# A decode kernel (attention with a cache, and a mixer MLP): weight loads moved in the DMA order, four column tiles with one fold, scores lagging four blocks

## Chip, cores, metric

One core of one Trainium2 chip. The metric is the device time of one execution in microseconds (us); lower is better. A "span" is the time from the first to the last instruction in the profile; it is about 1.7 us below the device time of the same run.

## The reference, cut to what matters

```python
x = A_x; xn = layernorm(x)                                   # 4 rows of 576
q = (xn @ wq)                                                # 32 heads of 128
k, v = last 2048 rows of the caches                          # 16 kv heads, 2 q heads each
attn = softmax(q k^T / sqrt(128)) v @ wo
h  = gelu(layernorm(xn) @ w1)                                # goes into zeros: S = 1, all four shifts are padding
x1 = xn + shifted(h) @ w2
mlp = x1 + gelu(layernorm(x1) @ w3) @ w4
out = x + attn + mlp
```

The data are 88.5 MB: K and V 33.6 MB each in 16 chunks of 2.097 MB, wq 4.7, w3 5.3, wo 4.7, w4 5.3, w1 and w2 1.3 together.

## The kernel before

Every operation is entered with a key, and each engine runs its operations in the order of the keys. PE (TensorE) is in order too: an operation that waits stops all behind it. This is what the argument needs:

```python
# --- DMA: the sync engine's queue unless engine= says otherwise ---
ev_x  = add_dma([(x_sb, x2)], "x", (), -100, engine="act")
ev_w1 = add_dma([(w1main, ...), (w1rag, ...)], "w1", (), -60)
ev_w2 = add_dma([(w2main, ...), (w2rag, ...)], "w2", (), -59)
ev_wq = [add_dma([(kt_t, ...)], "wq", (), -20), add_dma([(wqrag, ...)], "wqr", (), -15)]
for c in range(16):   # ring of 4 slots: chunk c waits until chunk c-4 has been transposed
    add_dma([(ring_pos(c), K chunk c)], ("k", c % 4), [t_done(c - 4)] if c >= 4 else [], c)
for c in range(16):   # V uses the same ring
    add_dma([(ring_pos(c), V chunk c)], ("v", c % 4), [f"PV{c-4}" if c >= 4 else t_done(c + 12)], KS + c)
ev_w3 = ... key W3_KEY = 140        # behind K15, ahead of V0 (KS = 144)
ev_wo = ... waits ["h2_4"], key KS + 15.5   # into w3's bytes, so w3 must have been read: behind V15
# w4 in five parts of 18, 10, 5, 2, 1 rows, behind wo

# --- PE, in the order of the keys ---
# xT(-40)  hs = hs_inT @ w2 (-39)  x2T(-36)  hT = w1.T xn2T (-35)  x1T(-34)  q = wq.T xnT (-30)  zeroing  K loop
for c in range(16):
    for k in range(8):                       # 8 blocks of 8 transposes, 4 PSUM buffers
        if k < 2 or k >= 4: wait(copy of the block four back)
        transpose block k                    # VectorE or ScalarE copies it out
        if k == 1: wait(copies 6 and 7 of chunk c-1); scores of chunk c-1   # SC_AFTER = 1
# max, exp, transposes of P, t1, then
# h2 = w3.T x1nT: 180 products (waits "PT3"), then 16 x PV
# AO: for r in 32: for h in 2: acc[h] += ORT[:, :, r].T @ wo[r, half h]      # 64 products, 4 stationary columns
# w4: for t in 36: for h in 2: acc[h] += h2T[:, t].T @ w4[t, half h]         # 72 products, 4 stationary columns
```

... (norms, masks, softmax details and the output are cut)

Of the kernel before, what the change touches and what calls it, by code (L numbers as in the profile page):

```python
# [5 lines left out]
FP32 = mybir.dt.float32  # L6
BF16 = mybir.dt.bfloat16
ACTF = mybir.ActivationFunctionType
ALU = mybir.AluOpType
AX = mybir.AxisListType  # L10
# [2 lines left out]
NPOS = 4  # L13
ACT_EVAC = (1, 4, 7)
N_WARM = 6
W3_KEY = 140.0
WO_AT = 15.5
W4_ROWS = (18, 10, 5, 2, 1)


# [14 lines left out]
def bass_parallel_sum__sliding_block_cached__mixer_s_mlp__decode_kernel(  # L35
    nc, A_x, A_k_cache, A_v_cache, A_wq, A_wo, B_x, B_w1, B_w2, B_w3, B_w4, out
):
    B, Sq, D = A_x.shape
# [10 lines left out]
    NBLK = NT // 8  # L49
# [3 lines left out]
    HALF = D // 2  # L53
# [6 lines left out]
    with ExitStack() as ctx:  # L60
        def sb(name, shape, dt):
            return ctx.enter_context(nc.sbuf_tensor(name, shape, dt))
# [9 lines left out]
        PT_t = sb("PT", [128, NT * 32], BF16)  # L72
# [4 lines left out]
        PTx = kt_t[:, 2048:4096].rearrange("p (q x) -> p q x", q=4)  # L77
# [4 lines left out]
        wo_v = w3_t[:, 0:32 * D].rearrange("p (r n) -> p r n", r=32)  # L82
        w3r = [w3_t[:, r * F:(r + 1) * F] for r in range(4)]
        w3rag = w3_t[:, 4 * F:4 * F + FH]
        w1main = w4_t[:, 0:4 * D].rearrange("p (r n) -> p r n", r=4)
        w1rag = w4_t[:, 4 * D:4 * D + HALF]
        w2main = w4_t[:, 5 * D:9 * D].rearrange("p (r n) -> p r n", r=4)
        w2rag = w4_t[:, 9 * D:9 * D + HALF]
# [13 lines left out]
        x1nT = sb("x1nT", [128, 6, B], BF16)  # L102
        hs_inT = sb("hs_inT", [128, 6, B], BF16)
        hT_sb = sb("hT_sb", [128, len(HCH), B], BF16)
        h2T_sb = sb("h2T_sb", [128, 36, B], BF16)
# [5 lines left out]
        permT_bf = sb("permT_bf", [128, 128], BF16)  # L111
        ident_f = sb("ident_f", [128, 128], FP32)
# [4 lines left out]
        zeros_bf = sb("zeros_bf", [128, 512], BF16)  # L117
# [7 lines left out]
        OTy = sb("OTy", [128, B, 32], BF16)  # L125
        ORT = sb("ORT", [128, B, 32], BF16)
        t1 = sb("t1", [B, D], FP32)
        out_sb = x1n_bf

        ps = ctx.enter_context(nc.psum_tensor("ps", [128, 8, 512], FP32))[:]  # L130
# [3 lines left out]
        ORps = ps[:, 2, 0:128]  # L134
        rinvps = ps[:, 3, 0:128]
        OTps = ps[:, 6, 0:32]
        H2Tps = ps[:, 7, 0:144].rearrange("p (c b) -> p c b", b=B)
        QTps = ps[:, 7, 0:128]
        HSps = [ps[0:B, k, 0:HALF] for k in range(2)]
# [10 lines left out]
        def add(engine, emit, waits=(), sig=None, key=0.0, inc=(), loop=None, cond=None):  # L150
            seqc[0] += 1
            prog[engine].append(Op(emit, waits, sig, key, seqc[0], inc, loop, cond))
# [6 lines left out]
        def take(nm, n=1):  # L159
            return ("take", tok(nm), n)  # L160

        def add_dma(pairs, skey, waits=(), key=0.0, engine="sp"):
            tok(skey)
            dma_count[skey] = dma_count.get(skey, 0) + 16 * len(pairs)

            def emit(e):
                for o_, i_ in pairs:
                    e.dma_start(o_, i_).then_inc(S[skey], 16)
            add(engine, emit, waits, None, key)
            return ("dma", skey, dma_count[skey])  # L170

        def rag_src(w_ap):
            return w_ap[512:576, :].rearrange("r (h n) -> (r h) n", h=2)

        KS = float(NB + 16)
# [26 lines left out]
            add("dve", lambda e, x=x: e.tensor_copy(out=mU_bf[:, :, x], in_=mU[:]), waits=["mU"], sig=f"mU_bf{x}", key=-7.8)  # L202


        ev_x = add_dma([(x_sb[:], x2)], "x", (), -100, engine="act")
        ev_w1 = add_dma([(w1main, B_w1[0:512, :].rearrange("(p r) n -> p r n", r=4)), (w1rag, rag_src(B_w1))], "w1", (), -60)
        ev_w2 = add_dma([(w2main, B_w2[0:512, :].rearrange("(p r) n -> p r n", r=4)), (w2rag, rag_src(B_w2))], "w2", (), -59)
        ev_wq = [add_dma([(kt_t[:], A_wq[0:512, :].rearrange("(p r) n -> p (r n)", r=4))], "wq", (), -20),
                 add_dma([(wqrag, rag_src(A_wq))], "wqr", (), -15)]

# [122 lines left out]
        def pe_SC(c):  # L333
            def f(e):
                ins = None
                for q in range(4):
                    for u in range(NU):
                        ins = e.matmul(Sps[32 * u:32 * u + 32, q, :].rearrange("p (t i) -> p t i", t=16),  # L338
                                       lhsT=Qs[:, c % NPOS, 32 * u:32 * u + 32], rhs=ktgrp[:, 4 * (c % 2) + q, :, u, :],
                                       start=False, stop=True, tile_position=(0, 32 * u), skip_group_check=True)  # L340
                return ins
            return f

        SC_AFTER = 1
        evtok = lambda k: take("evA" if k in ACT_EVAC else "evD")
        for c in range(NC):
            lp = ("K", c // NPOS)
            for k in range(NBLK):
                w = [take(("k", c % NPOS), 16)] if k == 0 else []
                prev = (k + 4) % 8  # L350
                if k < 2 or k >= 4:
                    w.append(evtok(prev))
                add("pe", pe_T(NBLK * c + k), waits=w, sig=f"T{NBLK * c + k}", key=NBLK * c + k, loop=lp)
                eng, f = evac(NBLK * c + k)
                add(eng, f, waits=[f"T{NBLK * c + k}"] + ([f"SC{c - 2}"] if c >= 2 else []), inc=[("evA" if eng == "act" else "evD", 1)],
                    key=NBLK * c + k + 0.2)
            add("pe", pe_SC(c - 1), waits=[evtok(6), evtok(7), take("qs")], sig=f"SC{c - 1}", key=NBLK * c + SC_AFTER + 0.5, loop=lp)
            b, gq = CH[c]
            cc = 4 * b + gq
            P(lambda e, c=c, cc=cc: e.tensor_copy(out=Qs[:, c % NPOS, :], in_=Qpad_t[:, 128 * cc:128 * cc + 128]),  # L360
              waits=["qT", "qs_zero"] + ([f"SC{c - NPOS}"] if c >= NPOS - 1 else []), inc=[("qs", 1)], key=c)
# [12 lines left out]
        for q in range(4):  # L374
            k0 = KS + 0.2 + 0.1 * q
            add("dve", lambda e, q=q: e.transpose(out=PTx[:, q, :], in_=P_sb[:, q, :]), waits=[f"exp{q}"], sig=f"PTx{q}", key=k0)  # L376
            add("pe", lambda e, q=q: e.matmul(ps[:, 4 + q, :], lhsT=permT_bf[:], rhs=PTx[:, q, :], start=True, stop=True),  # L377
                waits=[f"PTx{q}", "permT_bf"], sig=f"PTy{q}", key=k0)
            add("act", lambda e, q=q: e.activation(out=PT_t[:, 512 * q:512 * (q + 1)], in_=ps[:, 4 + q, :], func=ACTF.Copy),
                waits=[f"PTy{q}"], sig=f"PT{q}", key=k0 + 0.16)  # L380
        add("dve", lambda e: e.tensor_reduce(out=rsum[:], in_=rs4[:], axis=AX.X, op=ALU.add), waits=["exp3"], sig="rsum", key=KS + 0.8)
        add("dve", lambda e: e.reciprocal(out=rinv[:], in_=rsum[:]), waits=["rsum"], sig="rinv", key=KS + 0.81)
# [37 lines left out]


        def acc_mm(e, h, lhsT, rhs, start=False, stop=False):
            return e.matmul(ACC[h], lhsT=lhsT, rhs=rhs, start=start, stop=stop)  # L423

        def pe_AO(e):
            ins = None
            for r in range(32):
                for h in range(2):
                    ins = acc_mm(e, h, ORT[:, :, r], wo_v[:, r, HALF * h:HALF * (h + 1)])
            return ins  # L430
        KH = -58.0
        add("dve", lambda e: e.transpose(out=OTy[:].rearrange("p b r -> p (b r)"), in_=OTn[:]), waits=["OTn3"], sig="OTy", key=KT - 3)  # L432
# [45 lines left out]
        def pe_h2(r):  # L478
            def f(e):
                ins = None  # L480
                for n, (lo, hi, st) in enumerate(w4cols):
                    if r < 4:
                        ins = e.matmul(H2Tps[:, n, :], lhsT=w3r[r][:, lo:hi:st], rhs=x1nT[:, r, :],  # L483
                                       start=(r == 0 and n == 0), stop=False, skip_group_check=True)
                    else:
                        h = lo // FH
                        ins = e.matmul(H2Tps[:, n, :], lhsT=w3rag[:, lo - FH * h:hi - FH * h:st], rhs=x1nT[:, 4 + h, :],
                                       start=False, stop=True, skip_group_check=True)
                return ins
            return f  # L490
        for r in range(5):
            add("pe", pe_h2(r), waits=[ev_w3[r // 4]] + (["x1nT", "PT3"] if r == 0 else []), sig=None if r == 3 else f"h2_{r}",
                inc=[("otn", 1)] if r == 3 else [], key=KS + 2 + 0.1 * r)
        add("act", lambda e: e.activation(out=h2T_sb[:], in_=H2Tps, func=ACTF.Gelu_apprx_tanh), waits=["h2_4"], sig="gelu2", key=KS + 3)

        last_p = len(W4N) - 1
        for n, (t0, t1_) in enumerate(W4N):
            def f(e, t0=t0, t1_=t1_, hs=(0, 1), n=n):
                ins = None
                for t in range(t0, t1_):  # L500
                    for h in hs:
                        ins = acc_mm(e, h, h2T_sb[:, t, :], w4tile[t][:, HALF * h:HALF * (h + 1)], stop=(t == 35))
                return ins
            if n < last_p:
                add("pe", f, waits=[ev_w4[n], "gelu2"], sig=f"MO{n}", key=KT + 20 + n)
            else:
                for h in range(2):
                    add("pe", lambda e, f=f, h=h: f(e, hs=(h,)), waits=[ev_w4[n], "gelu2"], sig=f"MOl{h}", key=KT + 20 + n + 0.1 * h)
        add("dve", lambda e: e.tensor_copy(out=out_sb[:, 0:HALF], in_=ACC[0]), waits=["MOl0"], sig="fin0", key=KT + 50)  # L509
        add("act", lambda e: e.activation(out=out_sb[:, HALF:D], in_=ACC[1], func=ACTF.Copy), waits=["MOl1"], sig="fin1", key=KT + 50)  # L510

# [103 lines left out]
```

## Time and profile before

| | before |
|---|---|
| device time | 233.9 us (232.87 to 234.39, 3 runs) |
| profiled run | 236.5 us, span 234.8 |
| bytes at the V phase's rate (428.6 GB/s) | 206.5 us |
| end of the stream of loads | about 224.1 us |

The profile's lines are in the prediction below. The DMA row shows that the kernel is a stream of loads with a hole near 137 us and a tail of 10.7 us without loads. One more view: the timeline of the first 60 us of the kernel before. Columns of the timeline: start, length, engine, line, instruction, count, and in brackets the idle time before it and what ended it.

```profile
8.23 0.56 PEld L461 LDWEIGHTS ps<-w,hs_inT 128*4 128x4 bf16 x4 [2.56 <-DMA w<-in_B_w_dram]
...
34.14 25.23 SPq L168 DMA_DIRECT2D ring<-in_A_k_cache_dram  x5
```

The product with w2 (hs) starts at 8.23. K4 is issued at 34.14, when chunk 0 has been transposed; this moment is called T(0) below.

### The profile page before, as it was taken

The page shows a single profiled execution, that of the slowest core. Times are in us where ns is not written, and L with a number is a line of the kernel's source. Part 1 is how long each engine was busy: PE and PEld are TensorE (multiplying, and loading weights), DVE is VectorE, ACT ScalarE, POOL GpSimd, SP SyncE. Part 2 cuts the span into 40 slices and gives each one's busy share as a digit, 9 for nine tenths or more (in the row PEclk, how much of TensorE's full clock was granted, in tenths as well). Part 3 has the DMA queues.
Part 4 walks back from the last instruction along what each step waited for, and adds up shares of the span by engine and source line. Part 5 has one row for each costly group of instructions (what it writes and reads, how often), then busy time and mean ns, then how long its engine had stood idle before and what let it go on. Part 6 is the DMA issues. An engine that isn't in the chain of part 4 may idle for free. (4 is left out here: it accounts for less than half of the span.)

```text
span 234.8 us, 6313 instructions
## 1 busy us (share of the span) xinstructions
PE 156.7 (67%) x2874; PEld 126.0 (54%) x2876; DVE 75.5 (32%) x147; ACT 59.4 (25%) x71; POOL 10.6 (5%) x35
## 2 busy tenths in 40 slices
PE   0519898599989999999619996334433344306996
PEld 0218377477777777777504996334433344303664
DVE  4521165436665566666564002000110100100000
ACT  2020056246566555656656000000000000000000
POOL 8100000000000000000000000000000000000000
PEclk9999999979999999999965555555555555555999
DMA  6999999988999999999899919999999999999910
GB/s 202 432 392 437 430 424 422 395 332 329 402 388 399 366 371 363 392 461 446 374 442 436 413 56 396 430 438 422 433 441 416 433 424 430 474 394 421 409 40 1
DMA packets 6659, 88.67 MB, mean 378 GB/s; under 512 B 748, under 2 KB 1144, under 8 KB 1912
## 3 DMA queue, kind: packets, MB, share of 16 engines
q1 hardware_dynamic: 6632, 88.50, 91.5%
q8 instruction: 9, 0.15, 0.2%
q14 instruction: 2, 0.02, 0.0%
q10 hardware_dynamic: 16, 0.01, 0.0%
HBM read 88.49 MB, written 0.00 MB: 377 GB/s over the span
## 5 line engine op out<-in xcount | busy, mean ns | idle before, releaser
L331 DVE COPY kt<-ps 128x1024 bf16<-128x1024 bf16 x80 | 52.3, 687 | 39.7 <-PE ps L324 38.0
L324 PEld LDWEIGHTS ps<-perm_bf,ring 128*128 128x128 bf16 x1024 | 58.8, 99 | 11.5 <-issue 11.1
L324 PE MATMUL ps<-perm_bf,ring 128*128 128x128 bf16 x1024 | 62.4, 222 | 2.9 <-issue 2.7
L330 ACT ACTIVATE kt<-ps 128x1024 bf16<-128x1024 bf16 x48 | 47.9, 1024 | 53.3 <-PE ps L324 53.3
L406 PE MATMUL ps<-PTpad,ring 128*128 128x8 bf16 x1024 | 29.1, 168 | 37.6 <-PEq L533 37.6
L406 PEld LDWEIGHTS ps<-PTpad,ring 128*128 128x128 bf16 x1024 | 28.4, 104 | 38.3 <-issue 38.3
L510 ACT ACTIVATE x1n_bf<-ps 4x288 bf16<-4x288 f32 x1 | 0.4, 400 | 94.5 <-PE ps L423 94.5
L338 PE MATMUL ps<-kt,Qs 128*32 128x512 bf16 x272 | 18.9, 399 | 7.2 <-PEq L533 7.2
L395 DVE TENSOR_TENSOR PTpad<-PT,mU_bf 128x512 bf16<-128x512 bf16 x16 | 6.4, 422 | 40.5 <-PE ps L406 40.5
L423 PE MATMUL ps<-w,ORT 128*4 128x288 bf16 x64 | 10.4, 336 | 8.1 <-issue 8.1
L338 PEld LDWEIGHTS ps<-kt,Qs 128*32 128x32 bf16 x272 | 6.7, 98 | 13.6 <-issue 10.6
L423 PEld LDWEIGHTS ps<-w,ORT 128*4 128x4 bf16 x64 | 6.3, 100 | 12.0 <-issue 8.3
L418 DVE TENSOR_TENSOR OTn<-ps,rinvB 128x32 bf16<-128x32 f32 x4 | 0.8, 192 | 31.2 <-PE ps L406 31.2
L509 DVE CAST x1n_bf<-ps 4x288 bf16<-4x288 f32 x1 | 0.4, 445 | 26.9 <-PE ps L423 26.9
L423 PE MATMUL ps<-w,h2T_sb 128*4 128x288 bf16 x72 | 9.0, 286 | 0.0
L360 POOL COPY Qs<-Qpad 128x128 bf16<-128x128 bf16 x16 | 4.6, 296 | 86.6 <-PE ps L338 70.3
L483 PEld LDWEIGHTS ps<-x1nT,w 128*128 128x128 bf16 x144 | 8.0, 154 | 1.0 <-issue 1.0
L483 PE MATMUL ps<-x1nT,w 128*128 128x4 bf16 x144 | 8.1, 194 | 0.0
L423 PEld LDWEIGHTS ps<-w,h2T_sb 128*4 128x4 bf16 x72 | 6.1, 85 | 2.7
L285 PE MATMUL ps<-xnT,kt 128*128 128x4 bf16 x128 | 3.6, 166 | 4.0 <-DMA kt<-in_A_wq_dram 4.0
L285 PEld LDWEIGHTS ps<-xnT,kt 128*128 128x128 bf16 x128 | 3.5, 104 | 4.1 <-DMA kt<-in_A_wq_dram 4.1
L377 PE MATMUL ps<-kt,permT_bf 128*128 128x512 bf16 x3 | 1.8, 607 | 4.9 <-DVE kt L376 4.8
(93 smaller groups left out, 62.9 us busy)
## 6 DMA issues: line engine op xcount, KB each, us to landing
ring<-in_A_k_cache_dram SPq DMA_DIRECT2D x16, 2048.0 KB, 10.6
ring<-in_A_v_cache_dram SPq DMA_DIRECT2D x16, 2048.0 KB, 17.6
w<-in_B_w_dram SPq DMA_DIRECT2D x1, 4608.0 KB, 20.8
w<-in_A_wo_dram SPq DMA_DIRECT2D x1, 4608.0 KB, 27.9
kt<-in_A_wq_dram SPq DMA_DIRECT2D x1, 4096.0 KB, 15.2
w<-in_B_w_dram SPq DMA_DIRECT2D x1, 2592.0 KB, 33.5
w<-in_B_w_dram SPq DMA_DIRECT2D x3, 576.0 KB, 5.1
w<-in_B_w_dram SPq DMA_DIRECT2D x1, 1440.0 KB, 36.4
```

Of the source, the lines that this page charges most:

```text
L285: ins = e.matmul(QTps[:, B * h:B * (h + 1)], lhsT=w, rhs=x_, start=(r == 0 and h == 0), stop=(r == 4), skip_group_check=True)
L324: ins = e.transpose(tb[n % 4][:, t, :], slot_t(c)[:, 8 * k + t, :], perm_bf[:])
L330: return "act", lambda e: e.activation(out=ktbuf[:, n % 16], in_=tb[n % 4], func=ACTF.Copy)
L331: return "dve", lambda e: e.tensor_copy(out=ktbuf[:, n % 16], in_=tb[n % 4])
L338: ins = e.matmul(Sps[32 * u:32 * u + 32, q, :].rearrange("p (t i) -> p t i", t=16), lhsT=Qs[:, c % NPOS, 32 * u:32 * u + 32], rhs=ktgrp[:, ...
L360: P(lambda e, c=c, cc=cc: e.tensor_copy(out=Qs[:, c % NPOS, :], in_=Qpad_t[:, 128 * cc:128 * cc + 128]), waits=["qT", "qs_zero"] + ([f"SC{ ...
L377: add("pe", lambda e, q=q: e.matmul(ps[:, 4 + q, :], lhsT=permT_bf[:], rhs=PTx[:, q, :], start=True, stop=True), waits=[f"PTx{q}", "permT_ ...
L395: return lambda e: e.tensor_tensor(out=PTpad[:, c % 2], in0=PTv[:, :, cc, :].unsqueeze(2).to_broadcast([128, NT, NU, 2]), in1=mU_bf[:].uns ...
L406: ins = e.matmul(o_, lhsT=slot_t(c)[:, t, :], rhs=PTpad[:, c % 2, t].rearrange("p u e -> p (u e)"), start=(t == 0), stop=(t == NT - 1))
L418: add("dve", lambda e, hv=hv: e.tensor_tensor(out=hv(OTn), in0=OTps.rearrange("p (b h) -> p b h", b=B), in1=hv(rinvB), op=ALU.mult), waits ...
L423: return e.matmul(ACC[h], lhsT=lhsT, rhs=rhs, start=start, stop=stop)
L483: ins = e.matmul(H2Tps[:, n, :], lhsT=w3r[r][:, lo:hi:st], rhs=x1nT[:, r, :], start=(r == 0 and n == 0), stop=False, skip_group_check=True)
```

## The change

Its intent: keep the stream full. wq starts at once because w1 and w2 go to the scalar engine's queue; w3 comes early so that most of h2 can be done beside the softmax; wo comes among the V chunks so that AO need not wait; AO and most of w4 run in four column tiles; the scores no longer wait for the last copies.

```diff
-W3_KEY = 140.0      # behind K15
-WO_AT = 15.5        # behind V15
+W3_KEY = 13.5       # between K13 and K14
+WO_AT = 3.5         # between V3 and V4
-ev_w1 = add_dma([...], "w1", (), -60)
-ev_w2 = add_dma([...], "w2", (), -59)
+ev_w1 = add_dma([...], "w1", (), -60, engine="act")
+ev_w2 = add_dma([...], "w2", (), -59, engine="act")
-SC_AFTER = 1        # and T blocks 2, 3 without a wait, scores wait for copies 6 and 7
+SC_AFTER = 3        # every T block waits for the copy four back, scores for none
-add("pe", pe_h2(r), waits=[w3] + (["x1nT", "PT3"] if r == 0 else []), key=KS + 2 + 0.1 * r)
+add("pe", pe_h2(r), waits=[w3] + (["x1nT"] if r == 0 else []), key=KS + (0.01 + 0.01*r if r < 2 else 2 + 0.1*r))
+ACC4[h][32*u : 32*u+4] += ...   with tile_position=(0, 32*u), u = r % 4     # AO and the first 28 of 36 w4 rows
+acc_sb = copy of ACC4 (VectorE and ScalarE);  acc[h] += fold_f.T @ acc_sb   # fp32, once
```

... (zeroing of ACC4, PSUM banks of the P transposes and fold_f's making are cut)

More of the change, by code (lines that the diff above doesn't have):

```diff
@@ L15 @@
 N_WARM = 6
-W3_KEY = 140.0
-WO_AT = 15.5
+W3_KEY = 13.5
+WO_AT = 3.5
+N_FOLD = 2
 W4_ROWS = (18, 10, 5, 2, 1)
@@ L127, in bass_parallel_sum__sliding_block_cached__mixer_s_mlp__decode_kernel @@
         t1 = sb("t1", [B, D], FP32)
+        fold_f = sb("fold_f", [128, B], FP32)
+        acc_sb = sb("acc_sb", [128, D], FP32)
         out_sb = x1n_bf
@@ L136, in bass_parallel_sum__sliding_block_cached__mixer_s_mlp__decode_kernel @@
         OTps = ps[:, 6, 0:32]
+        ACC4 = [ps[:, 4 + k, 0:HALF] for k in range(2)]
         H2Tps = ps[:, 7, 0:144].rearrange("p (c b) -> p c b", b=B)
@@ L202, in bass_parallel_sum__sliding_block_cached__mixer_s_mlp__decode_kernel @@
             add("dve", lambda e, x=x: e.tensor_copy(out=mU_bf[:, :, x], in_=mU[:]), waits=["mU"], sig=f"mU_bf{x}", key=-7.8)
+        add("dve", lambda e: e.tensor_reduce(out=fold_f[:], in_=ident_f[:].rearrange("p (u x) -> p x u", u=4)[:, 0:B, :], axis=AX.X, op=ALU.add),
+            waits=["ident_f"], sig="fold_f", key=-8)
         ev_x = add_dma([(x_sb[:], x2)], "x", (), -100, engine="act")
-        ev_w1 = add_dma([(w1main, B_w1[0:512, :].rearrange("(p r) n -> p r n", r=4)), (w1rag, rag_src(B_w1))], "w1", (), -60)
-        ev_w2 = add_dma([(w2main, B_w2[0:512, :].rearrange("(p r) n -> p r n", r=4)), (w2rag, rag_src(B_w2))], "w2", (), -59)
+        ev_w1 = add_dma([(w1main, B_w1[0:512, :].rearrange("(p r) n -> p r n", r=4)), (w1rag, rag_src(B_w1))], "w1", (), -60, engine="act")
+        ev_w2 = add_dma([(w2main, B_w2[0:512, :].rearrange("(p r) n -> p r n", r=4)), (w2rag, rag_src(B_w2))], "w2", (), -59, engine="act")
         ev_wq = [add_dma([(kt_t[:], A_wq[0:512, :].rearrange("(p r) n -> p (r n)", r=4))], "wq", (), -20),
@@ L350, in bass_parallel_sum__sliding_block_cached__mixer_s_mlp__decode_kernel @@
                 prev = (k + 4) % 8
-                if k < 2 or k >= 4:
-                    w.append(evtok(prev))
+                w.append(evtok(prev))
                 add("pe", pe_T(NBLK * c + k), waits=w, sig=f"T{NBLK * c + k}", key=NBLK * c + k, loop=lp)
@@ L356, in bass_parallel_sum__sliding_block_cached__mixer_s_mlp__decode_kernel @@
                     key=NBLK * c + k + 0.2)
-            add("pe", pe_SC(c - 1), waits=[evtok(6), evtok(7), take("qs")], sig=f"SC{c - 1}", key=NBLK * c + SC_AFTER + 0.5, loop=lp)
+            add("pe", pe_SC(c - 1), waits=[take("qs")], sig=f"SC{c - 1}", key=NBLK * c + SC_AFTER + 0.5, loop=lp)
             b, gq = CH[c]
@@ L376, in bass_parallel_sum__sliding_block_cached__mixer_s_mlp__decode_kernel @@
             add("dve", lambda e, q=q: e.transpose(out=PTx[:, q, :], in_=P_sb[:, q, :]), waits=[f"exp{q}"], sig=f"PTx{q}", key=k0)
-            add("pe", lambda e, q=q: e.matmul(ps[:, 4 + q, :], lhsT=permT_bf[:], rhs=PTx[:, q, :], start=True, stop=True),
-                waits=[f"PTx{q}", "permT_bf"], sig=f"PTy{q}", key=k0)
-            add("act", lambda e, q=q: e.activation(out=PT_t[:, 512 * q:512 * (q + 1)], in_=ps[:, 4 + q, :], func=ACTF.Copy),
+            add("pe", lambda e, q=q: e.matmul(ps[:, 4 + q % 3, :], lhsT=permT_bf[:], rhs=PTx[:, q, :], start=True, stop=True),
+                waits=[f"PTx{q}", "permT_bf"] + (["PT0"] if q == 3 else []), sig=f"PTy{q}", key=k0)
+            add("act", lambda e, q=q: e.activation(out=PT_t[:, 512 * q:512 * (q + 1)], in_=ps[:, 4 + q % 3, :], func=ACTF.Copy),
                 waits=[f"PTy{q}"], sig=f"PT{q}", key=k0 + 0.16)
@@ L422, in acc_mm, with acc4_mm, pe_zero4 @@
         def acc_mm(e, h, lhsT, rhs, start=False, stop=False):
-            return e.matmul(ACC[h], lhsT=lhsT, rhs=rhs, start=start, stop=stop)
+            return e.matmul(ACC[h], lhsT=lhsT, rhs=rhs, start=start, stop=stop, skip_group_check=True)
+        def acc4_mm(e, n, h, lhsT, rhs):
+            u = n % 4
+            return e.matmul(ACC4[h][32 * u:32 * u + B, :], lhsT=lhsT, rhs=rhs, start=False, stop=True,
+                            tile_position=(0, 32 * u), skip_group_check=True)
+        def pe_zero4(e):
+            ins = None
+            for h in range(2):
+                ins = e.matmul(ACC4[h], lhsT=zeros_bf[:, 0:128], rhs=zeros_bf[:, 0:HALF], start=True, stop=True)
+            return ins
+        add("pe", pe_zero4, waits=["PT1", "PT3"], sig=None, key=KS + 1.3)
         def pe_AO(e):
             ins = None
-            for r in range(32):
+            for r0 in range(0, 32, 4):
                 for h in range(2):
-                    ins = acc_mm(e, h, ORT[:, :, r], wo_v[:, r, HALF * h:HALF * (h + 1)])
+                    for r in range(r0, r0 + 4):
+                        ins = acc4_mm(e, r, h, ORT[:, :, r], wo_v[:, r, HALF * h:HALF * (h + 1)])
             return ins
@@ L491, in bass_parallel_sum__sliding_block_cached__mixer_s_mlp__decode_kernel @@
         for r in range(5):
-            add("pe", pe_h2(r), waits=[ev_w3[r // 4]] + (["x1nT", "PT3"] if r == 0 else []), sig=None if r == 3 else f"h2_{r}",
-                inc=[("otn", 1)] if r == 3 else [], key=KS + 2 + 0.1 * r)
+            add("pe", pe_h2(r), waits=[ev_w3[r // 4]] + (["x1nT"] if r == 0 else []), sig=None if r == 3 else f"h2_{r}",
+                inc=[("otn", 1)] if r == 3 else [], key=KS + (0.01 + 0.01 * r if r < 2 else 2 + 0.1 * r))
         add("act", lambda e: e.activation(out=h2T_sb[:], in_=H2Tps, func=ACTF.Gelu_apprx_tanh), waits=["h2_4"], sig="gelu2", key=KS + 3)
@@ L499, in f @@
                 ins = None
-                for t in range(t0, t1_):
+                for tt in range(t0, t1_, 4):
                     for h in hs:
-                        ins = acc_mm(e, h, h2T_sb[:, t, :], w4tile[t][:, HALF * h:HALF * (h + 1)], stop=(t == 35))
+                        for t in range(tt, min(tt + 4, t1_)):
+                            w = w4tile[t][:, HALF * h:HALF * (h + 1)]
+                            ins = acc4_mm(e, t, h, h2T_sb[:, t, :], w) if n < N_FOLD else acc_mm(e, h, h2T_sb[:, t, :], w, stop=(t == 35))
                 return ins
@@ L508, in bass_parallel_sum__sliding_block_cached__mixer_s_mlp__decode_kernel, with pe_fold @@
                     add("pe", lambda e, f=f, h=h: f(e, hs=(h,)), waits=[ev_w4[n], "gelu2"], sig=f"MOl{h}", key=KT + 20 + n + 0.1 * h)
+        add("dve", lambda e: e.tensor_copy(out=acc_sb[:, 0:HALF], in_=ACC4[0]), waits=[f"MO{N_FOLD - 1}"], sig="acc0", key=KT + 40)
+        add("act", lambda e: e.activation(out=acc_sb[:, HALF:D], in_=ACC4[1], func=ACTF.Copy), waits=[f"MO{N_FOLD - 1}"], sig="acc1", key=KT + 40)
+        def pe_fold(e):
+            ins = None
+            for h in range(2):
+                ins = acc_mm(e, h, fold_f[:], acc_sb[:, HALF * h:HALF * (h + 1)])
+            return ins
+        add("pe", pe_fold, waits=["acc0", "acc1", "fold_f"], sig="fold", key=KT + 20 + N_FOLD + 0.5)
         add("dve", lambda e: e.tensor_copy(out=out_sb[:, 0:HALF], in_=ACC[0]), waits=["MOl0"], sig="fin0", key=KT + 50)
```

## The prediction

> **What bounds the kernel now.** I read, in this order, the page's slices, the stretches cut at the phases, the waits of the DMA queue, the timeline, and the chain that ended last.
>
> ```profile
> span 234.8 us, 6313 instructions
> PEclk9999999979999999999965555555555555555999
> DMA  6999999988999999999899919999999999999910
> ```
>
> The DMA row is near full in 36 of 40 slices, so the kernel is first of all a stream of 88.5 MB. It has one hole (slice 24) and a tail of about 1.5 slices without DMA. The granted clock is half from slice 22 to 37. The stretches give the sizes (columns: stretch, length, busy of PE, PEld, DVE, ACT, POOL, clock, DMA share, GB/s):
>
> ```profile
> 0.00:8.00 8.00, 0.31 (x6) 0.26 (x6) 4.43 (x15) 1.69 (x3) 5.97 (x19) 1.00 0.80 269
> 44.00:60.00 16.00, 12.65 (x185) 9.97 (x183) 8.14 (x13) 7.48 (x9) 0.59 (x2) 0.89 0.88 352
> 60.00:100.40 40.40, 37.34 (x628) 31.17 (x629) 25.11 (x40) 22.78 (x24) 2.37 (x8) 1.00 1.01 383
> 135.00:141.00 6.00, 6.00 (x180) 6.00 (x179) 0.42 (x1) 0.29 (x1) 0.00 (x0) 0.50 0.23 79
> 141.00:200.70 59.70, 23.94 (x840) 23.21 (x837) 5.56 (x16) 0.00 (x0) 0.00 (x0) 0.50 1.01 428
> 224.20:234.80 10.60, 8.38 (x69) 5.61 (x66) 0.45 (x1) 0.40 (x1) 0.00 (x0) 1.00 0.01 3
> ```
>
> In the V phase seven V chunks are issued between 155.44 and 184.80, so one chunk (2.097 MB) takes 4.89 us, 428.6 GB/s. At that rate 88.5 MB need 206.5 us. The stream ends at about 224.1, so 17.6 us are lost: 3.0 in the first 8 us (8 x (1 - 269/428.6)), 2.9 in 44 to 60, 4.3 in 60 to 100.4, 4.9 in 135 to 141, the rest scattered. Then 10.7 us follow without DMA. Who holds the stream back in K is seen in the DMA queue's waits and in one chunk of the timeline:
>
> ```profile
> SPq L168 <- PE ps L324: 107.0, 16, 27.7
> 60.13 0.58 PEld L338 LDWEIGHTS ps<-kt,Qs 128*32 128x32 bf16 x16 [0.58 <-issue]
> 60.16 1.05 PE L338 MATMUL ps<-kt,Qs 128*32 128x512 bf16 x16 [0.44 <-PEq L533]
> 61.14 3.60 PEld L324 LDWEIGHTS ps<-perm_bf,ring 128*128 128x128 bf16 x64 [0.42 <-issue]
> 65.32 0.58 PEld L338 LDWEIGHTS ps<-kt,Qs 128*32 128x32 bf16 x16 [0.58 <-issue]
> ```
>
> The queue waits for transposes to free a ring slot. A K chunk takes PE 65.32 - 60.13 = 5.19 us, more than its 4.89 us of DMA, and 0.58 of it is PE idle before the scores, which wait for ScalarE's copy of block 7. The hole and the tail:
>
> ```profile
> 135.66 2.05 PEld L487 LDWEIGHTS ps<-x1nT,w 128*128 128x128 bf16 x36
> 139.54 21.32 SPq L168 DMA_DIRECT2D ring<-in_A_v_cache_dram  x7
> 205.62 7.77 issue
> 213.39 19.21 PE ps L423 x136
> ```
>
> V4 cannot be issued before the first PV is done (139.54), which stands behind the 180 h2 products (127.74 to 137.63). At the end PE is ready at 205.62, waits 7.77 us for wo, then runs 136 products of four stationary columns, to 232.6.
>
> **What the Trainium skill says.** "DMA: Bandwidth & Descriptors", section Specifications, gives a fabric ceiling of 435 GB/s and about 358 per core for HBM; the V phase's 428 agrees with the first and is above the second, so I use 428.6. Its section "Issuing engines are not separate DMA queues" says that issuing from several engines saves only issue time; so w1 and w2 on ScalarE's queue save some issue time and no bandwidth. "TensorEngine Tiling (Array Packing)", section Key Properties, says that column tiles work independently and that changing the mode drains the array. The trace agrees with the first: 16 products of 512 columns in four tiles take 1.05 us[...]. "TensorE: Matmul & The Clock Gate", Part 1, says that the clock is half until about 3.4 us of activity; here the wo products run 0.24 us apart from 213.4 and 0.12 after about 218.2, 4.8 us later, while the 10 us of h2 and 7 us of PV never released it.
>
> **Start.** wq is issued at 0.8 in place of 2.68. The first 8 us lose about 2.0 in place of 3.0, so I put everything 1 us earlier: the last transpose of chunk 0, T(0), at 33.2 in place of 34.14. w1 and w2 share the engines with wq and land some 2 us later, still before wq is used.
>
> **K chunks.** Scores move from behind block 1 to behind block 3. Each transposed block waits for the copy four blocks back, 0.27 us after that copy's end. With 0.45 per block, copies of 0.69 (VectorE) and 1.02 (ScalarE), and results 0.2 after a block's end: the copy of block 4 ends 1.67 after block 4's start, so block 0 of the next chunk starts at 1.94 in place of 1.80. All others are ready, and the scores' two waits are gone. Chunk = 8 x 0.45 + 0.98 (scores, incl. drains) + 0.14 to 0.17 = 4.75 us, below 4.89: the stream is the bound now. In the first pass PE stops 2.7 us in the middle of a group (44.1 to 46.8, released by "issue") and runs cold after it; T(3) came 4.0 late. I keep these 4 us. T(2) = 33.2 + 9.5 + 2.9 = 45.6, T(3) = 51.4, T(9) = 33.2 + 42.75 + 4 = 79.95.
>
> Stream: 2.5 lost at first, 6.05 MB of small weights (14.1), so chunks 0 to c-1 are through at 16.6 + 4.89c. K6 needs T(2) and 1.5 to start: 47.1 for 45.9, 1.2 lost; K7 52.9 for 52.0, 0.9 lost. K12 is through at 16.6 + 63.6 + 2.1 = 82.3, K13 at 87.2.
>
> **w3 between K13 and K14** (5.31 MB, 12.4 us): w3 through at 99.6, K14 104.5, K15 109.4, V0 to V3 128.9. PE has done K13 at 98.95 and must wait for K14, landed 1.7 later at 106.2: about 7 us idle, then a cold chunk, 4.75 + 1.3. T(14) = 112.2, T(15) = 117.0, against 115.93 before. K is no earlier at its end, though faster.
>
> **From there to the restart.** Before, the scores ended at 118.30, 2.4 after T(15), and h2 at 137.63, 19.3 later. Now 72 of 180 h2 products (10.0/180 = 0.0555 each, 4.0 us) run while VectorE finds the maximum and ScalarE starts exp: before, the first transposing product came 4.1 after the scores, so they just fit. Two zeroing products and steps cost 0.7. 19.3 - 4.0 + 0.7 = 16.0; h2 is done at 117.0 + 2.4 + 16.0 = 135.4. Only then may wo be issued. V3 was through at 128.9: **a hole of 7 to 8 us stays**, not smaller than before.
>
> After the hole the same bytes are left in both kernels: 12 V (58.7 us), wo 4.72 MB (11.0), w4 5.31 MB (12.4), 82.1 us. Before: V4 issued 139.54 + 2.4 (start and scattered losses) + 82.1 = 224.1. Now 135.4 + 2.4 + 82.1 = **219.9**, 4.2 earlier.
>
> **Tail.** wo is long there. V15 is through at E = 219.9 - 12.4 = 207.5; PV and turning take 5.0 as before (200.7 to 205.7). AO: 64 products in 16 groups of four tiles at 0.24 cold, 3.9: E + 8.9. First w4 part (landed E + 7.8), 10 groups, half cold: E + 10.6. Second part landed E + 11.2, 6 groups at 0.12: E + 12.1 with latency. Two copies of 128x288 beside each other, 0.45 and semaphores: E + 12.7. Fold, two fp32 products; the fp32 adds of t1 took 2.08 cold for both, so 1.05 warm: E + 13.8. The 16 plain products that are left, 0.12 each, with latency: E + 16.0. The last w4 part lands at E + 14.1, so the tail is PE's by under 2 us: 223.5. Cast and output 2.3 as before (232.5 to 234.8): span 225.8, 9.0 less. The median is 0.9 under that span: **225.0 us**. Of the 9.0, 4.2 come from the restart and 4.8 from the shorter tail.
>
> **Rivals.** (A) The hole closes, if the chain from K15 to h2 is shorter than I think or PE gets K14 earlier: up to 7.5 less, 217.5. For it: scheduling w3 early is made for this. Against: K14 stands behind 12.4 us of w3 and PE has three chunks, 14 us, to bridge 17.3 + 4.9 us. (B) The clock stays at half through the tail, since groups of four small tiles count as little activity, like h2 and PV: AO, w4, fold and the rest end at E + 19.4, 228.5. Against: the same wo products did release it. (C) Column tiles do not overlap for four columns: AO 10, w4 as before plus the fold end at about E + 25.7, 234.7, nothing gained. Against: the scores' 1.05 us. (D) The stop of 2.7 us at "issue" falls away or a second one comes: 2 less or 3 more.
>
> **Range and chances.** D and the size of the hole give about 3 to either side, A pulls down, B up by 3.4. Range 219.5 to 229.5. Faster by over 2% is under 229.2: chance 0.87. Within 2%, which needs B with a longer hole, or C: 0.11. Slower 0.02.
>
> **What would show it.** Pitch of the scores in K about 4.75 to 4.9, no idle of 0.58 before them; K13 to K14 a PE wait of some 7 us with the clock falling; 72 h2 products before the exponentials' transposes; a hole in the DMA row of 7 to 8 us near 130, ended by wo's issue at about 135; no wait before AO, AO in about 4 us; end of the stream near 220 and of the span near 226. It is wrong if the stream restarts before 132 or after 139, if AO takes over 6 us, or if the end lies more than 8 us behind the stream's end.

## The result, and the profile after

247.55 us (244.21 to 248.83, 4 runs) against 234.14 (232.87 to 234.91) of the kernel before: slower, ratio 1.0531, 95% interval 1.0412 to 1.0649. Ratios here and below are the mean time of one kernel's runs over the mean of the other's of the same rounds, so not quite the ratio of the medians. Executions over 1.5% slower than the fastest of the same kernel are left out of the means.

The page of the changed kernel: rows of 40 slices (clock and DMA share in tenths), then the DMA queues (packets, MB, share) and the chain that ended last.

```profile
span 247.0 us, 6332 instructions
...
PEclk9999999998599999999858955555555555555579
DMA  7999980098589999999999990589999999999990
...
q1 hardware_dynamic: 6056, 87.17, 84.7%
q10 hardware_dynamic: 592, 1.33, 1.4%
...
DMA 11%; PE 2%; SPq 1%; ACT 0%; issue 0%
```

The stream now has two holes: a new one in slices 7 and 8 (counted from 1, as in the prediction), and the old one, now in slices 25 and 26. At the end the chain is DMA and no longer PE. The timeline of the changed kernel (columns as before) shows what stands in the first hole:

```profile
28.78 0.56 PEld L480 LDWEIGHTS ps<-w,hs_inT 128*4 128x4 bf16 x4 [22.43 <-DMA w<-in_B_w_dram]
...
34.42 3.57 PE L292 MATMUL ps<-xnT,kt 128*128 128x4 bf16 x128
...
48.48 0.54 SPq L172 DMA_DIRECT2D ring<-in_A_k_cache_dram  x1
```

hs starts at 28.78 in place of 8.23: PE had waited 22.43 us for a B weight, w2. q follows at 34.42, though wq had long landed (its main part was issued at 0.81 and landed 13.5 us later). T(0) is 48.48. The ring of four was full by 36, so the stream stood still until T(0) freed a slot:

```profile
36.00:40.00 4.00, 4.00 (x111) 3.17 (x109) 1.11 (x9) 0.29 (x3) 0.56 (x3) 1.00 0.07 25
40.00:44.00 4.00, 3.85 (x16) 1.40 (x15) 0.81 (x2) 0.00 (x0) 0.20 (x1) 1.00 0.00 0
44.00:48.00 4.00, 4.00 (x72) 3.25 (x70) 2.39 (x4) 1.88 (x2) 0.30 (x1) 1.00 0.02 4
...
148.00:152.00 4.00, 4.00 (x28) 1.94 (x28) 0.96 (x3) 1.55 (x2) 0.00 (x0) 0.50 0.17 74
152.00:156.00 4.00, 4.00 (x76) 4.00 (x75) 0.00 (x0) 0.00 (x0) 0.00 (x0) 0.50 0.02 4
```

(The last three columns are clock, DMA share and GB/s.) The later part of the changed kernel's timeline:

```profile
126.36 3.57 PE L331 MATMUL ps<-perm_bf,ring 128*128 128x128 bf16 x32 [9.68 <-PEq L563]
...
140.81 4.11 PE L502 MATMUL ps<-x1nT,w 128*128 128x4 bf16 x72
...
156.90 0.33 SPq L172 DMA_DIRECT2D w<-in_A_wo_dram  x1
...
233.63 4.02 PE L433 MATMUL ps<-w,ORT 128*4 128x288 bf16 x64 [0.38 <-DVE ORT L454]
```

PE waits 9.68 us for K14, which stands behind w3; 72 h2 products run beside the search for the maximum; wo is issued at 156.90 when h2 is done, after a hole of about 9 us; before AO, PE is idle for only 0.38 us, until VectorE has copied its operand, and AO takes 4.02 us. In the kernel before it waited 8.11 us for wo ("issue" here) and took 10.38:

```profile
213.39 10.38 PE L423 MATMUL ps<-w,ORT 128*4 128x288 bf16 x64 [8.11 <-issue]
```

The end of the span is 6.0 us behind the stream's end (about 241.0) in place of 10.7.

### The profile page after: what moved, and what is told of

The parts are those of the page before. It is cut to its first block, busy times and chain, and to the rows that moved or that the text cites. A ratio compares the mean times of both kernels' runs of the same rounds, so it can differ in the third digit from the quotient of the medians.

```text
span 247.0 us, 6332 instructions
## 1 busy us (share of the span) xinstructions
PE 149.2 (60%) x2882; PEld 120.8 (49%) x2882; DVE 75.6 (31%) x149; ACT 59.7 (24%) x72; POOL 10.6 (4%) x35
## 3 DMA queue, kind: packets, MB, share of 16 engines
q10 hardware_dynamic: 592, 1.33, 1.4%
## 5 line engine op out<-in xcount | busy, mean ns | idle before, releaser
L331 PE MATMUL ps<-perm_bf,ring 128*128 128x128 bf16 x1024 | 64.5, 226 | 14.9 <-PEq L563 9.7
L331 PEld LDWEIGHTS ps<-perm_bf,ring 128*128 128x128 bf16 x1024 | 61.0, 101 | 23.3 <-issue 23.2
L480 PE MATMUL ps<-w,hs_inT 128*4 128x288 bf16 x8 | 2.3, 438 | 22.4 <-DMA w<-in_B_w_dram 22.4
L480 PEld LDWEIGHTS ps<-w,hs_inT 128*4 128x4 bf16 x8 | 0.8, 116 | 23.1 <-DMA w<-in_B_w_dram 22.4
L345 PEld LDWEIGHTS ps<-kt,Qs 128*32 128x32 bf16 x272 | 5.9, 98 | 7.5 <-issue 2.7
L486 DVE TENSOR_TENSOR x_bf<-ps,xn_bf 4x288 bf16<-4x288 f32 x2 | 0.9, 446 | 22.1 <-PE ps L481 22.1
L257 ACT ACTIVATE sd<-mv 4x1 f32<-4x1 f32 x3 | 0.6, 202 | 27.9 <-DVE mv L255 27.9
L433 PE MATMUL ps<-w,ORT 128*4 128x288 bf16 x64 | 4.0, 443 | 0.4 <-DVE ORT L454 0.4
L271 PE MATMUL ps<-ident_bf,xn_bf 4*128 4x4 bf16 x8 | 0.6, 170 | 6.1 <-POOL ident_f L187 6.1
## 6 DMA issues: line engine op xcount, KB each, us to landing
ring<-in_A_k_cache_dram SPq DMA_DIRECT2D x16, 2048.0 KB, 10.7
w<-in_B_w_dram SPq DMA_DIRECT2D x1, 4608.0 KB, 21.2
kt<-in_A_wq_dram SPq DMA_DIRECT2D x1, 4096.0 KB, 13.5
```

What stands on the lines that cost most here:

```text
L331: ins = e.transpose(tb[n % 4][:, t, :], slot_t(c)[:, 8 * k + t, :], perm_bf[:])
L345: ins = e.matmul(Sps[32 * u:32 * u + 32, q, :].rearrange("p (t i) -> p t i", t=16), lhsT=Qs[:, c % NPOS, 32 * u:32 * u + 32], rhs=ktgrp[:, ...
L433: return e.matmul(ACC4[h][32 * u:32 * u + B, :], lhsT=lhsT, rhs=rhs, start=False, stop=True, tile_position=(0, 32 * u), skip_group_check=True)
L480: e.matmul(HSps[h], lhsT=hs_inT[:, r, :], rhs=w2main[:, r, HALF * h:HALF * (h + 1)], start=(r == 0), stop=False)
```

## The experiments

Theory A: the loss is the start. w2's packets on the second queue take turns with the large packets of wq and K, so w2 lands late, and PE, in order, cannot do q before it. Rival W: the loss is w3 ahead of K14. Every kernel below gave a correct result.

**e2: the kernel before with w1 and w2 alone moved.**

```diff
-... "w1", (), -60)                 -... "w2", (), -59)
+... "w1", (), -60, engine="act")   +... "w2", (), -59, engine="act")
```

> The kernel before with nothing but w1 and w2 moved to the scalar engine's queue. Theory A: w2 lands near 28, chunk 0 is transposed about 14 us later than 34.1, DMA stands still from about 36 until then, and the time is 245 to 249. Rival W: no w3 is moved here, so the time stays at 234 within 1%.

Measured: 249.14 us, ratio 1.0642 (1.054 to 1.0745). hs started at 28.8 and T(0) was 48.3, as in the changed kernel:

```profile
28.81 0.56 PEld L461 LDWEIGHTS ps<-w,hs_inT 128*4 128x4 bf16 x4 [21.84 <-DMA w<-in_B_w_dram]
```

This one part of the change makes the kernel before at least about as slow as the whole change does (1.0642 and 1.0531, with intervals that overlap). Rival W as the cause of the slowdown is out.

**e1: the changed kernel with w1 and w2 back on the sync queue.** The edit is e2's reversed.

> The changed kernel, with w1 and w2 again first on the sync engine's queue. Theory A (w2 lands late because its packets take turns with wq and K packets, and PE, in order, cannot do q before it): hs starts near 8.2 us and the last transpose of chunk 0 comes at 34 in place of 48.5, some 14 us earlier, and the span falls from 247 to 229 to 233. Rival W (w3 in front of K14 is the cause, PE waits 9.8 us for K14): the start is put right but the span stays above 240.

Measured: 230.75 us, ratio 0.9865 (0.9802 to 0.9927), span 230.8. hs at 7.6, T(0) at 32.07. Theory A holds in both directions: where w1 and w2 go decides the start. (How w2 comes to be late is the question of e3 and e10.) But the rest of the change, which I had put at nearly 4%, brings 1.4% (0.7 to 2.0). PE still waits 10.2 us for K14, and from 131 to 141 the stream moves 43 GB/s:

```profile
7.62 0.57 PEld L480 LDWEIGHTS ps<-w,hs_inT 128*4 128x4 bf16 x4 [1.24 <-DMA w<-in_B_w_dram]
...
109.98 3.57 PE L331 MATMUL ps<-perm_bf,ring 128*128 128x128 bf16 x32 [10.25 <-PEq L563]
...
131.00:141.00 10.00, 10.00 (x142) 7.75 (x142) 1.09 (x4) 2.45 (x4) 0.00 (x0) 0.50 0.10 43
```

**e3 and e10: is it turns by packet?** Each DMA engine has 36 packets of w1 and w2 in the changed kernel (592 on q10, less the 16 that q10 has before, over 16 engines). e3 leaves the main parts on the scalar queue and puts the ragged rows at the head of the sync queue. e10 (on the base of e4 below) moves w2 alone and leaves w1 at the head of the sync queue. Both have 18 packets per engine on the scalar queue, but 1.19 and 0.67 MB.

```diff
# e3                                                      # e10
-add_dma([(w1main..), (w1rag..)], "w1", engine="act")     -add_dma([(w2main..), (w2rag..)], "w2", (), -59)
+add_dma([(w1main..)], "w1", engine="act")                +add_dma([(w2main..), (w2rag..)], "w2", (), -59, engine="act")
+add_dma([(w1rag..)], "w1r", (), -58)     # sync; w2 alike
```

> The changed kernel; the main parts of w1 and w2 stay on the scalar engine's queue, their ragged rows (72 KB each, 128 packets each) go at the head of the sync engine's queue. Theory A (turns by packet, whatever their bytes): the 16 main packets of each DMA engine take turns with the 16 small ragged ones, so hs starts before 11 us and chunk 0 is done near 34 to 36; span 229 to 235. Rival B (the scalar engine's queue gets a small share of the bytes or waits for what was queued before it): 1.18 of 1.33 MB are still there, hs starts after 20 us, and the span is above 240.

> As e4, but w2 alone goes to the scalar engine's queue while w1 stays at the head of the sync queue, so two queues of equally small packets start side by side (some 18 packets per DMA engine each) and wq comes behind w1. Theory A (turns by packet): w2 takes turns with w1's small packets, hs starts between 6 and 10 us, chunk 0 is done at 30 to 32, time within 1 us of e4. Rival B (a second queue is always late): hs starts after 14 us and the time rises by 4 us or more.

The page's queue line and the timeline's first hs, of e3:

```profile
q10 hardware_dynamic: 304, 1.19, 1.3%
...
16.73 0.57 PEld L482 LDWEIGHTS ps<-w,hs_inT 128*4 128x4 bf16 x4 [11.06 <-DMA w<-in_B_w_dram]
```

and of e10:

```profile
q10 hardware_dynamic: 304, 0.67, 0.8%
...
16.46 0.57 PEld L480 LDWEIGHTS ps<-w,hs_inT 128*4 128x4 bf16 x4 [10.79 <-DMA w<-in_B_w_dram]
```

Both numbers that I expected of theory A were missed: hs came at 16.7 and 16.5, not before 11 or 10. (e3 took 234.62 us in one run, span 232.9; e10 226.14 us, ratio 0.9641, by the medians 3.5 us above e4's code on the same chip, by the means 4.0.) So e10 came out about as its rival, "a second queue is always late", had said, and only what the packets did can tell the two theories apart.

I had counted on the small packets at the head of the sync queue as partners in the turns. The traces also keep a record of every packet (trace.npz; no prof view lists them). In e3, 223 of the 256 ragged packets have started by 3.0 us, when 15 of the scalar queue's have, so most were gone. In both runs about half of the scalar queue's 18 packets per engine start before wq's packets of 32 KB take over (wq's first starts at 4.1 us in e3, at 5.2 in e10), and the other half start between wq's, until 16 us.

What the pair shows: **the same number of packets lands at the same time, though the bytes differ by 1.8**, and twice the packets (28.78) take 12.2 us longer. By itself the pair leaves a rival: e3 and e10 have two weight transfers on the scalar queue and the changed kernel has four, so turns by whole transfer would fit too. The packet records of the changed kernel settle it. From 17 to 22 us 99 packets of 16 KB start on the sync queue and 116 of 4.6 KB on the scalar queue, from 23 to 27 us 98 of 16 KB and 111 of 0.58 KB: the two queues go forward nearly packet for packet, whatever the packets hold. 12.2 us for 18 packets are 0.68 us per turn. A packet of a K chunk, one partition's row of 16 KB, takes 0.61 us of it (median in the records). A share by bytes (rival B) would have given e3 and e10 different landings.

The Trainium skill, "DMA: Bandwidth & Descriptors", section Queues, rings and completion order, says that each DMA engine goes round the queues with work and takes one whole packet of each. (It puts a packet at some 9 to 17 descriptors; in the records here a turn is one partition's row.) I had read another section of that page and drawn an even share of bytes from it; the packet records show 1.33 MB against 9.7 MB of the other queue by 28.8 us.

**e4: as e1, with w3 again behind K15.**

```diff
-W3_KEY = 13.5
+W3_KEY = 140.0
```

> As e1 (w1 and w2 first on the sync queue), and w3 again behind K15 as in the kernel before; wo among the V chunks, column tiles and the later scores stay. If w3 in front of K14 costs what the trace suggests (PE waits about 10 us for K14, and the hole of 7 to 9 us in the stream follows from it): no PE wait in K, h2 is done near 131, the stream runs through without a hole over 3 us, and the span is 219 to 224. If the place of w3 does not matter: the same as e1 within 1%.

Measured: 221.91 us, ratio 0.9473 (0.9355 to 0.9591), span 219.2; by the means 4.2% below e1 on the same chip (221.2 and 231.0). The stretches of e4:

```profile
60.00:107.00 47.00, 47.00 (x804) 39.30 (x801) 32.87 (x52) 29.65 (x30) 2.05 (x7) 1.00 1.01 429
107.00:132.00 25.00, 20.97 (x401) 17.06 (x400) 7.99 (x15) 8.73 (x16) 0.00 (x0) 0.56 1.01 426
132.00:212.00 80.00, 29.89 (x945) 26.74 (x949) 5.93 (x18) 0.00 (x0) 0.00 (x0) 0.52 1.00 425
```

There is no hole any more: the stream runs at 425 to 429 GB/s from 60 us on. wo is issued at 125.51, when h2 is done (I had expected about 131), 15 us earlier than in e1 (140.51). So the early place of w3 was a loss by itself, hidden in the result behind the larger one.

**e9: as e1, with w3 behind K6.** `W3_KEY = 6.5` in place of 13.5.

> As e1, with w3 behind K6 in place of K13. Theory (whatever stands before K15 in the stream delays K15's landing, and the softmax and h2 hang on that; where in K makes no difference): a PE wait of some 10 us near chunk 7 in place of 14, the same hole of 6 to 9 us before wo, span 227 to 232. Rival (only the late place hurts, an earlier w3 hides in K): no long PE wait, no hole, span under 223.

Measured: 226.11 us in one run of unknown state, span 224.4. PE waits 9.0 us near chunk 7 and the stream moves 139 GB/s from 128 to 138, which is about 6.8 us of hole. The mechanism is the theory's; the span is 2.6 us under its range (227 to 232). An earlier place may then cost less than K14's; one run on another chip does not show it.

**e8: as e4, with w1 and w2 on the sync queue behind wq** (keys -14 and -13 in place of -60 and -59), to start wq at once without a second queue.

> As e4, with w1 and w2 on the sync queue behind wq in place of before it. It keeps the intent of starting the large wq transfer at once, without two queues. In e4 the first 8 us lose about 3 us of the stream to small transfers. Theory: w2 lands near 17, chunk 0 is done at 32 to 34, still in time for the ring, and the span falls by 0.5 to 1.5 us. Rival (any late w2 stops PE): the K phase starts over 4 us later than in e4 (30.8) and the time rises by 2 us or more.

Measured: 228.53 us, ratio 0.9791 (0.9707 to 0.9876), "unclear" by the 2% rule against before. hs at 17.81, T(0) at 39.56, DMA at 25 GB/s from 36 to 40. My theory was wrong and its rival right, and here no second queue is involved: q does not run before hs in PE's order, so w2 late by 10 us puts T(0) 8.7 us later than in e4 (30.82).

**e5: the kernel before with the later scores alone.**

```diff
-SC_AFTER = 1 ; if k < 2 or k >= 4: w.append(evtok(prev)) ; scores wait evtok(6), evtok(7), qs
+SC_AFTER = 3 ; w.append(evtok(prev))                     ; scores wait qs
```

> The kernel before with nothing but the scores behind block 3. Theory: the K chunk falls from 5.19 to 4.68 us (as in the changed kernel's trace), K becomes bound by DMA, the last transposes come 5 to 8 us earlier than 115.9, h2 with w3 behind K15 is done near 130, the hole of 5 us in the stream shrinks to under 3 us; the tail stays 10.7 us. Time 225 to 229, faster by 2 to 4%. Rival: the PE gain in K is lost because DMA bounds K anyway: same within 1%.

Measured: 229.47 us, ratio 0.9891 (0.9812 to 0.9969). The chunk takes 4.68 us, V3 is issued at 107.29 in place of 115.93, V4 at 130.90 in place of 139.54. The mechanism came as expected (the stream moves 269 GB/s in the five us around V4's issue, 130 to 135, where the kernel before moves 79 from 135 to 141), but these are the profiled runs, the fastest of e5 (227.04) and a slow one of the kernel before, so they show the gain too large. It is 1.1% (0.3 to 1.9), half of what I expected or less. The rival, "same within 1%", is not excluded; no gain at all is.

**e6: the kernel before with column tiles and fold alone** (the last two lines of the change's diff).

> The kernel before with nothing but the column tiles and the fold. wo still lands at 213 and AO waits for it. Theory: AO takes about 4 us in place of 10, the end is then bound by the landing of w4 and the fold, PE ends at 228 to 230.5 in place of 232.5: time 229.5 to 232, 1 to 2% faster. Rival: tiles of four columns do not overlap, or the fold eats it: same within 0.5%.

Measured: 231.28 us, ratio 0.9933 (0.9876 to 0.9991), 0.7%: less than the 1 to 2% expected, and the rival's "same within 0.5%" is not excluded. The clock (third column from the right) stayed at half through most of the tail:

```profile
214.00:218.10 4.10, 4.02 (x64) 2.17 (x64) 0.00 (x0) 0.00 (x0) 0.00 (x0) 0.50 0.95 403
218.10:221.50 3.40, 1.31 (x36) 0.84 (x36) 0.00 (x0) 0.00 (x0) 0.00 (x0) 1.00 0.98 407
221.50:228.20 6.70, 4.52 (x34) 2.01 (x33) 0.46 (x1) 0.41 (x1) 0.00 (x0) 0.50 0.30 116
```

In the profiled run, the slowest of the five, the last 20 PE instructions of the chain that ended last take 4.56 us, where the same 20 of the changed kernel take 3.10.

**e7, and e11 with e12: as e4, with wo again last** (`WO_AT = 15.5`); e11 and e12 are the codes of e4 and e7 again, side by side.

> As e4, with wo again behind all V chunks. Theory (the stream has no hole in e4 and AO takes 4 us, so the place of wo is worth little): between 0.5 us less and 2.5 us more than e4, within 1%. Rival (wo among the V chunks is what saves the tail): 5 us or more above e4.

> The same code as e4, beside e10 and e12 on one chip, so that these three can be compared: 220 to 224 us.

> The same code as e7 (wo behind all V chunks), beside e4's code. In e7 the clock stayed at half through the tail: 20 products after the second w4 part took 5.1 us against 3.1 in e4. Theory: the early wo is worth about these 2 us, by keeping AO and w4 together so that the clock is released: 1 to 3 us above e11. Rival: no difference beyond 0.5 us, and e7 was another chip.

e7: 224.72 us, ratio 0.9658 (0.9601 to 0.9715), on another chip than e4. The timelines of the tail, of e4:

```profile
211.69 0.90 PE L433 MATMUL ps<-w,h2T_sb 128*4 128x288 bf16 x20 [1.27 <-DMA w<-in_B_w_dram]
213.91 1.39 PE L429 MATMUL ps<-w,h2T_sb 128*4 128x288 bf16 x10 [1.32 <-DMA w<-in_B_w_dram]
215.13 1.13 PE L429 MATMUL ps<-acc_sb,fold_f 128*4 128x288 f32 x4
```

and of e7:

```profile
211.08 1.60 PE L433 MATMUL ps<-w,h2T_sb 128*4 128x288 bf16 x20 [1.59 <-DMA w<-in_B_w_dram]
212.81 2.56 PE L429 MATMUL ps<-w,h2T_sb 128*4 128x288 bf16 x10
215.16 2.00 PE L429 MATMUL ps<-acc_sb,fold_f 128*4 128x288 f32 x4
```

With wo last, AO and the w4 products have a gap of 2.12 us between them, the clock is at half through most of the tail, and each group takes nearly twice as long. That is the one use of the early wo that the traces show. The gap alone does not decide it: e6 has the same gap (2.11), and there the clock was full from 218.1 to 221.5, as its lines above show. In time it is not settled: e11 gave 222.6 us (ratio 0.9566, 0.9492 to 0.9641) and e12 224.05 (0.9555, 0.9479 to 0.963), no difference outside the noise. The profiled runs alone (219.87 and 224.53) would have shown 2%, but they were the fastest of the one and the slowest of the other.

**What no run priced.** A sixth part of the change is hidden in the diff: 72 of the h2 products no longer wait for the softmax (`PT3`). It was never run alone. The code of e7 and e12 has the later scores, the column tiles and this part, and took 0.9658 and 0.9555 of the time before; the first two alone gave 0.9891 and 0.9933. From the last K chunk's transposes to the issue of V4 it took 21.0 us in e7 (105.59 to 126.62), against 23.6 in e5 (107.29 to 130.90) and in the kernel before (115.93 to 139.54). So this part likely makes a good share of the gain; no run of its own shows it.

## Why the prediction was wrong

The step that failed, in its words: "w1 and w2 share the engines with wq and land some 2 us later, still before wq is used." hs started 20.5 us later than before, and T(0), which the prediction put 1 us earlier, came 14.3 us later. The even sharing was assumed; neither the trace of the kernel before (whose second queue carried 16 packets) nor the section that I named says it. The prediction also failed to look at what stands in PE's order between w2 and q: hs, x2T, hT, x1T, all ahead of q. None of its rivals was about the start, so the range could not hold the result. e1 and e2 show it; the packet records with e3 and e10 show why w2 is late, and e8 shows that a late w2 holds q back. No run moved hs behind q in PE's order, which would test that half directly. Even with the start put right, e1's span (its slowest run) is 5.0 us above the predicted 225.8. There the mis-sized terms are w3 ahead of K14 (4.0: 41.08 for 37.05) and the first pass (2.2: 48.96 for 46.75), while the start is 1.1 us better; the table has them.

| | predicted | changed kernel | e1 |
|---|---|---|---|
| hs starts | about 10 | 28.78 | 7.6 |
| T(0) | 33.2 | 48.48 | 32.07 |
| K chunk | 4.75 | 4.68 | 4.68 |
| T(0) to T(9) | 46.75 | 49.50 | 48.96 |
| T(9) to T(15) | 37.05 | 40.52 | 41.08 |
| T(15) to wo's issue | 18.4 | 18.40 | 18.40 |
| wo's issue to stream's end | 84.5 | about 84.1 | about 84.1 |
| stream's end to end of span | 5.9 | 6.0 | 6.2 |
| span | 225.8 | 247.0 | 230.8 |

- **Start**: 15.3 of the 21.2 us by which the span was missed (48.48 - 33.2).
- **First pass of the K loop**: PE's stop cost T(3) 7.4 us in place of the 4.0 (T(1) 53.16, T(2) 63.41, T(3) 69.89, against a pitch of 4.68). The chunks' pitch was 0.07 us below the predicted one, so T(0) to T(9) came out 2.75 us longer. e1 has 8.31 and 7.0 us for the same two chunks, e4 8.2 and 6.25. It is no mark of the code: e11, which is e4's code, has 7.94 and 4.68. The packet records show what PE may wait for: in all 14 traces it goes on 1.2 to 1.4 us after the third 16 KB packet of the queue that the page calls "instruction" has landed (45.43 and 46.81 in the kernel before, 61.10 and 62.45 in the changed one). So it looks like a wait for instructions; no run tests it.
- **w3 ahead of K14**: right in kind (PE waits, the clock falls, the hole stays), wrong in size: PE waited 9.7 us and not 7, and the cold chunk took 7.5 us and not 6.05; 3.5 us.
- **From T(15) on**: right. The 72 h2 products fit beside the maximum, AO took 4.0 us (predicted 3.9), the stream's rest and the tail came within 0.4 us. Rival B (clock at half through the tail) was not true of the changed kernel; it is true of e7, and but for 3.4 us of e6, where wo stays last. What the prediction says of tiles agrees with its trace: four zeroing products of 512 columns without tiles take 1.91 us in the kernel before (at 25.78), so 16 would take 7.6, an estimate; 16 in tiles take 1.05, and 1.90 where the clock is half (changed kernel, at 129.86).
- **Later scores**: right in mechanism, and e5 gives their worth alone: 1.1%.

The prediction saw that "a hole of 7 to 8 us stays, not smaller than before" and did not draw the conclusion that w3's move was then a loss: 4.2% between e1 and e4. It compared the whole change with the kernel before, where each part should have been asked alone. The fastest code is e4's: later scores, column tiles, early wo and the split h2, with the loads of w1, w2 and w3 left as they were, 0.9473 and 0.9566 of the time before on two chips. The same with wo last (e7, e12) had 0.9658 and 0.9555, so the early wo is not shown to help.

## What to carry to other kernels

A load that the in-order PE needs early should not sit on a second DMA queue in small packets beside a deep queue of large ones: queues take turns by packet, so here it got bytes in the ratio of the packet sizes, and each of its packets cost a turn of 0.68 us. Nor should it stand behind a large load on the same queue (e8). Ahead of moving a load forward, ask what it delays in the same stream and whether a wait further on hangs on that; a stream that is full has no free place. When a change has several parts, price each alone, and for each DMA that moves follow the first instruction that waits for it in its engine's order.

## What the Trainium skill lacked or had wrong

- "DMA: Bandwidth & Descriptors", section Queues, rings and completion order, has the turns by packet, but not what they do to a small load: 36 packets per engine (1.33 MB) landed at 28.8 us and 18 packets at 16.5 to 16.7, whether 0.67 or 1.19 MB, 0.68 us per turn against packets of 16 KB. Its advice that queues on several engines only save issue time should say that it can cost: the same two loads let hs start at 8.2 us from the head of one queue and at 28.8 us from a second one.
- The same page, section Specifications, lists about 358 GB/s per core for HBM as a limit; e4, a program on one core, held 425 to 429 GB/s over 150 us. That is not new to the page: its section Bandwidth has 425 for one core alone and about 358 where both cores of an HBM domain stream.
- "TensorE: Matmul & The Clock Gate", Part 1, speaks of activity without saying what counts. Here 10 us of h2 products with four moving columns and the PV products left the clock at 0.5, while column-tiled products of 288 columns released it about 3.6 us (e4, 205.3 to 208.9) and 5.6 us (e11, 204.7 to 210.3) after AO began, where w4 followed closely. With a gap of 2.1 us behind 4.0 us of AO it stayed at half in e7 and e12, but was released in e6 at 218.1 for 3.4 us. What decides between these stays open.
- No page sizes PE's stop in the first pass of a loop: T(3) came 7.4 us late in the changed kernel, 4.0 in the kernel before, both released by "issue", and in all 14 traces PE went on 1.2 to 1.4 us after the third packet of the instruction queue.
